# A new written-out order for a two-layer linear-attention kernel, with the first loads dealt anew to two queues

## The chip, the cores and the metric

The kernel runs on one core of one Trainium2 chip. The metric is device time in microseconds (us), the median over runs of the same program. Smaller is better.

## What is computed

Two layers, each an attention block A and a gated block B, on 2048 rows of 512 features in bfloat16. Both layers use the same weights. The attention has 32 heads of 16 features and no softmax over rows: a feature map of keys and queries (two softmaxes over 16 features) turns it into products.

```python
def A(x, wqkv, w_phi, wo):                       # H = 32 heads, Dh = 16
    q, k, v = split_heads(x @ wqkv)
    pq, pk = q @ w_phi, k @ w_phi                # per head, 16 x 16
    phi_q = concat(softmax(pq), softmax(-pq))
    phi_k = concat(softmax(pk), softmax(-pk))
    kv, z = phi_k.T @ v, phi_k.sum(rows)         # over all 2048 rows
    return merge_heads(phi_q @ kv / (phi_q @ z + 1e-6)) @ wo

def B(x, W_gate, W_up, W_down):                  # 512 -> 1376 -> 512
    return (relu(x @ W_gate) * (x @ W_up)) @ W_down

x = A_x
for layer in range(2):
    x = x + A(layernorm(x), A_wqkv, A_w_phi, A_wo)
    x = x + B(layernorm(x), B_W_gate, B_W_up, B_W_down)
```

## The kernel before

The 2048 rows are 16 tiles of 128 rows (t0 to t15), in four chunks of four tiles. X stays in SBUF for the whole run. `w_phi` is folded into the key and query weights once at the start: VectorE spreads it into block matrices `Wblk` by two products (L269), TensorE multiplies them with the transposed key weights `wkT` in four folds b0 to b3 of four matmuls each (L287), and the results are evacuated into `Wk2` by ScalarE (L249) or VectorE (L251). The same is done later for the query weights (`Wq2`), whose transposing load is L279.

A tile's way through the start of a layer: VectorE takes statistics (L311, aggregated in L313), GpSimd makes the scalars (L319, L321 the power -1/2, L368, L370), ScalarE (L382) or VectorE or GpSimd (both L394) normalises, and the normalised tile is transposed, either by TensorE (L403, with an evacuation; only for t0) or by a transposing DMA on SyncE's queue (L412 for one tile, L408 for two at once). Then TensorE makes keys (L575) and values (L516), ScalarE two exponentials of the keys (L580), VectorE sums them over the features (L546, or L552 and L556 for halves) and inverts the sums, VectorE and GpSimd scale (L595), and TensorE adds the tile to the running product of keys and values (L617). After the last tile's keys the queries (L659, L663, L674, L681, turned by L683) meet that product (L700); the quotient (L718, L720) is turned by DMA (L727, L733) or TensorE (L740), projected (L751) and added to X (L420, L424). The next normalisation leads into block B: gate and up matmuls (L466), their evacuation and product (L476, L479), down projection (L498).

Nothing is ordered by the compiler. Every step is an operation of a planner (`Plan.op`) with an engine, and `ORDER` is a written-out permutation of all 1867 operations; each engine, SyncE's DMA queue included, executes its operations in that order. `STEP` holds letters and digits per tile that say which engine does a step: `xn1` normalises in layer 0, `xm0` ("2": two tiles turned by one DMA, "1": each by its own), `ks` (how many of eight head groups GpSimd scales), `kr` and `qr` (how sums are made), `sA` and `sB` (for how many chunks ScalarE's square replaces VectorE's statistics), `ot` (which engine turns the quotient), `wake` (dummy matmuls on zeros at the start, L260). The first loads are not in the order; they are issued at the head of `setup`.

By the numbering of the operations, the queues begin like this before the change (K and V are a tile's keys and values):

- TensorE: 8 dummies, fold b0, 2 dummies, fold b1, dummy, fold b3, transposition of t0, dummy, fold b2, dummy, V t0, dummy, K t0, dummy, V t1, K t1, K t2
- ScalarE: evacuate b0, normalise t0, normalise t1, evacuate t0's transposition, evacuate b1 and b2, normalise t2, both exponentials of t0, normalise t3 and t4, one exponential of t1, V t0, the other of t1, one of t3, V t1
- VectorE: statistics of t0, both `Wblk` products, statistics of t1, t3, t2, evacuate b3, statistics of t5, t4, t6
- GpSimd, around tiles 6 and 7: (scalars of t8/t9 and t6/t7 mixed) power of t9, power of t7, normalise t7, last scalar of t6/t7
- SyncE: t1, t2, t3, the pair t4/t5, the query weights, the pair t6/t7

Of the kernel before, what the change touches and what calls it, by code (L numbers as in the profile page):

```python
# [9 lines left out]
D = 512  # L10
# [123 lines left out]
WF_IN, WK_IN, WV_IN, WQ_IN, LOADED = 3.6, 5.6, 8.25, 13.0, 13.0  # L134
X_IN = [3.25, 5.2] + [6.75] * 2 + [9.75] * 4 + [11.25] * 4 + [12.75] * 4
# [8 lines left out]
def setup(ctx, tc, A_x, A_wqkv, A_w_phi, A_wo, B_W_gate, B_W_up, B_W_down, out):  # L144
    nc = tc.nc
    st = KS()
# [11 lines left out]
    pl = st.pl = Plan()  # L158
# [3 lines left out]
    X = const.tile([P, T, D], BF16, name="X")  # L162
    xv = xf.rearrange("(t p) d -> p t d", p=P)
# [3 lines left out]
    wf = const.tile([P, NDB, DH], BF16, name="wf")  # L167
    nc.sync.dma_start_transpose(out=wkT[:], in_=A_wqkv[:, D:2 * D])
    nc.scalar.dma_start(out=X[:, 0:1, :], in_=xv[:, 0:1, :])
# [7 lines left out]
    wake = const.tile([P, 1], F32, name="wake")  # L177
# [86 lines left out]
def feature_weights(st):  # L264

    nc, pl = st.nc, st.pl
# [6 lines left out]
    for name, dst, off, at in (("Wk2", st.Wk2, D, WK_IN), ("Wq2", st.Wq2, 0, WQ_IN)):  # L273
        pl.rank("w" if off else "wq")
        if off:
            part, deps = (lambda m, b: st.wkT[:, b, m * P:(m + 1) * P]), []
        else:
            wqT = Buf("b4", [P, NDB, D], BF16)
            pl.op("SP", 2.0, lambda: nc.sync.dma_start_transpose(out=wqT[:], in_=st.wq_in),  # L279
                  reads=[("turns", 1)], writes=[(wqT, 0)], at=at, lat=3.0)  # L280
            part, deps = (lambda m, b: wqT[:, b, m * P:(m + 1) * P]), [(wqT, 0)]
# [406 lines left out]
def attention(st, c, pT, norm, L):  # L688
# [71 lines left out]
    "part0": "4111", "part1": "4111", "tB0": "A---", "tB1": "D-D-", "tA": "----", "wev": "AADDAAADADAAAAAA",  # L760
    "xn1": "AAAAADAPDAADAAAA", "turn": "A---", "wake": 19, "fuse0": "FFFA", "fuse1": "AFFF", "gate": 1, "sB0": 4,
# [6 lines left out]
}  # L768
ORDER = (
# [176 lines left out]
```

## Time and profile before

| | |
|---|---|
| Runs | 384.75 us median of 3 (384.26 to 385.19) |
| Profiled execution | 384.6 us, span 382.9 us |
| Busy TensorE, VectorE, ScalarE, GpSimd | 366.5, 274.9, 199.9, 136.6 us |
| Granted TensorE clock, mean of the span | 1.00 |
| Packets moved by DMA | 100065, 31.82 MB |

The profile is of one execution. Times in it are us from the start of the span. In a row of the timeline the first number is the start, the second the duration, then come engine, line, operation, what is written and read, and in brackets how long the engine had been idle and what ended the wait. ACTq and SPq are the DMA queues of ScalarE and SyncE. Rows that overlap on one engine are pipelined.

### The profile page before, as it was taken

The numbers are of one execution on the slowest core, as the hardware profiler recorded it, in microseconds if no ns is written. First come the engines' busy times: TensorE is split into PE (matmuls) and PEld (weight loads), VectorE is DVE, ScalarE is ACT, GpSimd is POOL, SyncE is SP. The second block draws the span as 40 slices with busy tenths as digits, with TensorE's granted clock in tenths as the row PEclk, the third lists the DMA queues.
The fourth block names the chain that finished last, engine by engine and source line by source line (L and its number), as shares of the span: only waits on it lengthen the run. The fifth ranks groups of instructions, "written<-read, shape, count | busy, mean of one in ns | idle before, by whom it ended". The sixth has DMA issues, their size and how long they took to land.

```text
span 382.9 us, 6693 instructions
## 1 busy us (share of the span) xinstructions
PE 366.5 (96%) x2384; PEld 190.5 (50%) x2417; DVE 274.9 (72%) x601; ACT 199.9 (52%) x428; POOL 136.6 (36%) x281
## 2 busy tenths in 40 slices
PE   7978988989989999999999989999999999999997
PEld 3334454756544544444454445576554544454443
DVE  6999999998875775556787878999974746333432
ACT  3799866924377621333777556995635432332100
POOL 4799775914343001133361344374531202000000
PEclk9999999999999999999999999999999999999999
DMA  8699647443872520017302122364784221310004
GB/s 243 162 146 267 148 110 140 90 86 68 161 123 44 98 41 3 0 28 119 74 2 42 27 44 43 62 119 87 143 146 96 57 41 15 69 41 2 0 5 134
DMA packets 100065, 31.82 MB, mean 83 GB/s; under 512 B 91488, under 2 KB 100032, under 8 KB 100032
## 3 DMA queue, kind: packets, MB, share of 16 engines
q1 hardware_dynamic: 96832, 28.75, 38.8%
q10 hardware_dynamic: 3200, 2.64, 2.3%
q8 instruction: 19, 0.31, 0.4%
q14 instruction: 14, 0.11, 0.1%
HBM read 7.39 MB, written 2.10 MB: 25 GB/s over the span
## 4 chain that ended last, share of the span: by engine, by line
PE 81%; DMA 9%; ACT 2%; DVE 2%; issue 2%; POOL 2%; SPq 0%; ACTq 0%; POOLq 0%; DVEq 0%
PE ps L466 36%; PE ps L498 16%; DMA b<-b 7%; PE ps L751 7%; PE ps L575 5%; PE ps L659 5%; PE ps L516 5%; PE ps L446 2%; PE q L700 2%; PE q L617 1%; DMA wf<-in_A_w_phi_dram 1%; ACT b L580 1%; DVE sk L556 1%; ACT b L382 1%; POOL b L595 0%
## 5 line engine op out<-in xcount | busy, mean ns | idle before, releaser
L476 ACT CAST b<-ps 128x512 bf16<-128x512 f32 (+2 forms) x100 | 47.7, 505 | 69.3 <-PE ps L466 69.1
L466 PE MATMUL ps<-b,wu 128*128 128x512 bf16 (+2 forms) x400 | 79.5, 336 | 0.5 <-DMA b<-b 0.5
L466 PE MATMUL ps<-b,wg 128*128 128x512 bf16 (+2 forms) x400 | 79.7, 336 | 0.0
L498 PE MATMUL ps<-wd,b 128*128 128x512 bf16 (+3 forms) x365 | 79.1, 366 | 0.5
L479 DVE SCALAR_TENSOR_TENSOR b<-ps,b 128x512 bf16<-128x512 f32 (+2 forms) x70 | 40.5, 605 | 36.5 <-PE ps L466 25.5
L595 POOL TENSOR_TENSOR b<-b,rk 128x1024 bf16<-128x1024 bf16 (+7 forms) x30 | 41.0, 1381 | 45.0 <-DVE rk L589 30.4
L498 PEld LDWEIGHTS <-b 128*128 128x128 bf16 (+1 forms) x374 | 35.4, 98 | 39.1 <-issue 0.2
L466 PEld LDWEIGHTS <-wu 128*128 128x128 bf16 x400 | 35.9, 98 | 32.5 <-DMA b<-b 0.8
L466 PEld LDWEIGHTS <-wg 128*128 128x128 bf16 x400 | 35.8, 98 | 31.5
L580 ACT ACTIVATE b<-ps 128x512 bf16<-128x512 f32 x64 | 35.9, 613 | 16.2 <-PE ps L575 15.8
L382 ACT ACTIVATE b<-X,ve,rstd 128x512 bf16<-128x512 bf16 x39 | 31.6, 823 | 16.4 <-POOL ve L370 16.4
L663 ACT ACTIVATE b<-ps 128x512 bf16<-128x512 f32 x64 | 34.9, 615 | 8.3 <-PE ps L659 7.2
L681 POOL TENSOR_TENSOR b<-b,rq 128x512 bf16<-128x512 bf16 x24 | 25.4, 1068 | 30.1 <-DVE rq L674 29.6
L575 PE MATMUL ps<-Wk,b 128*128 128x512 bf16 x125 | 31.8, 379 | 4.6 <-DMA b<-b 4.4
L420 DVE SCALAR_TENSOR_TENSOR X<-ps,X 128x512 bf16<-128x512 f32 x36 | 24.3, 681 | 16.0 <-PE ps L498 8.3
L424 DVE TENSOR_TENSOR X<-X,ps 128x512 bf16<-128x512 bf16 (+2 forms) x30 | 19.3, 648 | 21.7 <-PE ps L498 16.1
L334 ACT ACTIVATE sq<-X 128x512 bf16<-128x512 bf16 x36 | 22.9, 636 | 18.8 <-DVE X L420 18.5
L516 PE MATMUL ps<-wvt,b 128*128 128x512 bf16 x124 | 31.8, 379 | 0.9 <-DMA b<-b 0.6
L751 PE MATMUL ps<-wo,b 128*128 128x512 bf16 x117 | 31.1, 379 | 0.7
L659 PE MATMUL ps<-Wq,b 128*128 128x512 bf16 x122 | 30.2, 379 | 0.3
L546 DVE TENSOR_REDUCE sq<-b 128x64 f32<-128x1024 bf16 x19 | 22.5, 1199 | 0.0
L720 DVE TENSOR_TENSOR b<-q,dd 128x512 bf16<-128x512 f32 x32 | 21.8, 681 | 0.3
(86 smaller groups left out, 444.7 us busy)
## 6 DMA issues: line engine op xcount, KB each, us to landing
out_dram<-X SPq DMA_DIRECT2D x15, 128.0 KB, 1.8
X<-in_A_x_dram ACTq DMA_DIRECT2D x3, 512.0 KB, 7.1
b<-b SPq DMA_TRANSPOSE x92, 3.1
wu<-in_B_W_up_dram SPq DMA_DIRECT2D x8, 160.0 KB, 3.4
wg<-in_B_W_gate_dram SPq DMA_DIRECT2D x8, 160.0 KB, 3.6
wd<-in_B_W_down_dram SPq DMA_DIRECT2D x5, 256.0 KB, 3.9
wvt<-in_A_wqkv_dram ACTq DMA_DIRECT2D x1, 512.0 KB, 5.1
wo<-in_A_wo_dram SPq DMA_DIRECT2D x4, 128.0 KB, 3.2
```

What stands on the lines that cost most here:

```text
L382: pl.op("ACT", 0.72, lambda to=to, t=t, j=j: nc.scalar.activation(out=to(), in_=st.X[:, t, :], func=AF.Identity, scale=rstd[:, j:j + 1], b ...
L466: nc.tensor.matmul(ps[:], lhsT=wt[:, b, f * P:(f + 1) * P], rhs=xnT[:, lo:hi, b, :], start=(b == 0), stop=(b == NDB - 1))
L476: pl.op("ACT", 0.065 + 0.42 * share, lambda ups=ups, ru=ru: nc.scalar.copy(out=ru[:], in_=ups[:]), reads=[(ups, 0)], writes=[(ru, 0)])
L479: pl.op("DVE", 0.08 + 0.53 * share, lambda gps=gps, ru=ru, h=h, cs=cs: nc.vector.scalar_tensor_tensor(out=h[:, cs], in0=gps[:], scalar=0.0 ...
L498: nc.tensor.matmul(yps[:], lhsT=hs[f][:fsz, ti * P:(ti + 1) * P], rhs=st.wd[:fsz, f, cols], start=(f == 0), stop=(f == NFT - 1))
L516: nc.tensor.matmul(vp[:], lhsT=xnT[:, ti, kb, :], rhs=st.wvt[:, kb, :], start=(kb == 0), stop=(kb == NDB - 1))
L575: nc.tensor.matmul(ps[:], lhsT=xnT[:, ti, kb, :], rhs=w(kb), start=(kb == 0), stop=(kb == NDB - 1))
L580: pl.op("ACT", 0.49, lambda s=s, ek=ek, pk=pk: nc.scalar.activation(out=ek[:, :, s, :], in_=pk[:].rearrange("p (j x) -> p j x", j=8), func ...
L595: eng.tensor_tensor(out=phiK[:, lo:hi, :, :].rearrange("p j s (f h) -> p (j s) f h", h=4), in0=ek[:, lo:hi, :, :].rearrange("p j s (f h) - ...
L659: nc.tensor.matmul(pq[:], lhsT=xnT[:, ti, kb, :], rhs=st.Wq2[:, kb, :], start=(kb == 0), stop=(kb == NDB - 1))
L663: pl.op("ACT", 0.49, lambda s=s, eq=eq, pq=pq: nc.scalar.activation(out=eq[:, :, s, :], in_=pq[:].rearrange("p (j x) -> p j x", j=8), func ...
L751: nc.tensor.matmul(yps[:], lhsT=turned(b), rhs=st.wo[:, b, :], start=(b == 0), stop=(b == NDB - 1))
```

## The change

The loads at the head of `setup`, the planner's arrival times, the duration of one planned DMA, the letters of `STEP` and the whole of `ORDER` are new. `ORDER` has 1863 operations now.

```diff
-WF_IN, WK_IN, WV_IN, WQ_IN, LOADED = 3.6, 5.6, 8.25, 13.0, 13.0
-X_IN = [3.25, 5.2] + [6.75] * 2 + [9.75] * 4 + [11.25] * 4 + [12.75] * 4
+WF_IN, WK_IN, WV_IN, WQ_IN, LOADED = 3.35, 6.0, 8.3, 13.0, 13.0
+X_IN = [3.1, 4.7] + [6.8] * 2 + [9.8] * 4 + [11.3] * 4 + [12.8] * 4
...
+    nc.sync.dma_start(out=X[:, 0:1, :], in_=xv[:, 0:1, :])
     nc.sync.dma_start_transpose(out=wkT[:], in_=A_wqkv[:, D:2 * D])
-    nc.scalar.dma_start(out=X[:, 0:1, :], in_=xv[:, 0:1, :])
     nc.scalar.dma_start(out=wf[:], in_=A_w_phi.rearrange("(b j) d f -> (j d) b f", b=NDB, j=8))
     nc.scalar.dma_start(out=X[:, 1:2, :], in_=xv[:, 1:2, :])
...
-            pl.op("SP", 2.0, lambda: nc.sync.dma_start_transpose(out=wqT[:], in_=st.wq_in),
-                  reads=[("turns", 1)], writes=[(wqT, 0)], at=at, lat=3.0)
+            pl.op("SP", 2.3, lambda: nc.sync.dma_start_transpose(out=wqT[:], in_=st.wq_in),
+                  reads=[("turns", 1)], writes=[(wqT, 0)], at=at, lat=2.9)
...
-    "part0": "4111", "part1": "4111", "tB0": "A---", "tB1": "D-D-", "tA": "----", "wev": "AADDAAADADAAAAAA",
-    "xn1": "AAAAADAPDAADAAAA", "turn": "A---", "wake": 19, "fuse0": "FFFA", "fuse1": "AFFF", "gate": 1, "sB0": 4,
-    "sB1": 3, "sA": 2, "xB0": "ADADDAADDADADDDD", "xB1": "DADAAADDAAAAADAA", "xA": "AADDDDDAAADAAAAA",
-    "xm0": "11222211", "xmB0": "12222112", "xmB1": "22222221", "xm1": "12221212", "om0": "11112222",
-    "om1": "11222222", "ev0": "AAAAAAAAAAAAAAAA", "ev1": "AAADDAADAAAAAAAA", "ks0": "7888076880873788",
-    "ks1": "4321818154616442", "kr0": "H112121121122222", "kr1": "P111121112122212", "qm0": "DPDDDDDDDDPDDDPD",
-    "qm1": "DDDDPPDDDDPDDPDD", "qr0": "2111H1122121P1PP", "qr1": "111P112122111112", "qs0": "PPPPPPPPDDDPDPPD",
-    "qs1": "DDPDPPPPPPPPPPPP", "ot0": "DDDD------DDAA--", "ot1": "--A-DDAD---DD--A",
+    "part0": "4111", "part1": "4111", "tB0": "A---", "tB1": "D-D-", "tA": "----", "wev": "ADDDAAADADAAAAAA",
+    "xn1": "AAAAADAPDAADAAAA", "turn": "A---", "wake": 18, "fuse0": "FFFA", "fuse1": "AFFF", "gate": 1, "sB0": 2,
+    "sB1": 3, "sA": 3, "xB0": "ADADDADDDADADDAD", "xB1": "DADAAADDDAAAADAA", "xA": "AADDDDDAAAAAAAAA",
+    "xm0": "21122111", "xmB0": "12222112", "xmB1": "22222221", "xm1": "11222212", "om0": "11112222",
+    "om1": "11222222", "ev0": "AAAAAAAAAAAAAAAA", "ev1": "AAADDADDAAAAAAAA", "ks0": "6888076880873788",
+    "ks1": "4322018154616442", "kr0": "H112121121122222", "kr1": "P111121112222212", "qm0": "DPDDDPDDDDPDDDPP",
+    "qm1": "DDDDPPDDDDPDDPDD", "qr0": "1111H1122121P1PP", "qr1": "1112112122111112", "qs0": "PPPPPPPPDDDPDPPP",
+    "qs1": "DDPDPPPDPDPPPPPP", "ot0": "DDDD------DDADAA", "ot1": "----DDAD---DA--A",
...
-    131, 144, 139, 143, 145, 129, 135, 130, 0, 1, 148, 149, 2, 3, 9, 4, 5, 150, 138, 10, 147, 152, 11, 13, 134, 12,
+    136, 140, 133, 145, 147, 131, 0, 138, 148, 1, 149, 146, 141, 137, 2, 132, 4, 3, 9, 10, 150, 5, 157, 153, 13,
...
```

By the numbering, the queues begin like this after it:

- TensorE: 12 dummies, folds b3, b1, b0, b2, transposition of t0, K t0, 3 dummies, V t0, K t1, V t1, K t2, V t2, K t3, dummy, K t4
- ScalarE: normalise t0, evacuate b0, b1, b2, normalise t1, evacuate t0's transposition, normalise t2 and t3, both exponentials of t0, normalise t4, V t0, one exponential of t1, V t1, normalise t6, the other of t1, one of t2, both of t3
- VectorE: statistics of t0, one `Wblk` product, statistics of t1, the other product, statistics of t2, t3, evacuate b3, statistics of t4, t5, t6
- GpSimd, around tiles 6 and 7: power of t7, last scalar of t6/t7, normalise t7, power of t9
- SyncE: t1, t2, t3, t5, t4, the query weights, the pair t6/t7

Counted over the whole run, TensorE loses one dummy and one transposition of a tile's quotient (`ot1`, t2), VectorE gains 9 operations (four more statistics with their aggregates among them), ScalarE loses 6, GpSimd 8, and SyncE gains 3 transposing DMAs.

184 rows, old and new, of the table ORDER are left out of this document.

## The prediction

> **What bounds the kernel now.** I read the page first, then the busy time of each engine in stretches of 10 us, then the timelines of the first 40 us engine by engine, and last the groups of instructions by line. From the page:
>
> ```profile
> span 382.9 us, 6693 instructions
> ...
> PE 366.5 (96%) x2384; PEld 190.5 (50%) x2417; DVE 274.9 (72%) x601; ACT 199.9 (52%) x428; POOL 136.6 (36%) x281
> ```
>
> TensorE is busy for 366.5 of 382.9 us, so all that any order can win from idle TensorE is 16.4 us. The stretches say where they lie (columns: us, then busy us of PE, PEld, DVE, ACT, POOL, with counts):
>
> ```profile
> 10.00:20.00 10.00, 9.07 (x40) 3.60 (x41) 9.28 (x25) 7.33 (x15) 7.18 (x18) 1.00 0.67 156
> ...
> 20.00:30.00 10.00, 8.27 (x54) 4.19 (x54) 9.39 (x19) 9.68 (x20) 9.35 (x17) 1.00 1.03 153
> ...
> 30.00:40.00 10.00, 8.89 (x67) 4.27 (x67) 9.89 (x15) 10.00 (x20) 9.90 (x6) 1.00 1.05 245
> ...
> 50.00:60.00 10.00, 8.73 (x99) 5.20 (x100) 10.00 (x16) 6.62 (x14) 7.65 (x8) 1.00 0.32 67
> ...
> 220.00:230.00 10.00, 8.88 (x71) 4.47 (x70) 7.64 (x15) 5.07 (x8) 4.90 (x16) 1.00 0.24 42
> ```
>
> In the stretches from 10 to 60 us TensorE is idle for 0.93, 1.73, 1.11 and 1.27 us, while VectorE is busy for 9.28 to 10.00 of each 10 us and ScalarE for up to 10.00. That is the key and query phase of layer 0: the vector engines set its pace, and TensorE waits for them. Between 220 and 230 us 1.12 us are lost, the most of any stretch after 110 us. So the change can win something in the first third, little after that, and it can lose anywhere.
>
> **The start: three loads and what hangs on them.** Timeline of the first 14 us (start, duration, engine, line):
>
> ```profile
> 0.78 0.39 ACTq L169 DMA_DIRECT2D X<-in_A_x_dram  x1
> ...
> 0.79 1.42 SPq L168 DMA_TRANSPOSE wkT<-in_A_wqkv_dram  x1
> ...
> 1.20 0.45 ACTq L170 DMA_DIRECT2D wf<-in_A_w_phi_dram  x1
> ...
> 1.24 3.60 PE L260 MATMUL ps<-zero 128*128 128x512 bf16 x8 [1.24 <-DVE zero L176]
> ...
> 5.32 0.19 POOL L370 TENSOR_TENSOR ve<-u,rstd 128x1 f32<-128x1 f32 x1
> ...
> 5.52 0.76 DVE L269 TENSOR_TENSOR Wblk<-M,wf 128x256 bf16<-128x256 bf16 x2 [1.16 <-DMA wf<-in_A_w_phi_dram]
> ...
> 6.20 0.69 DVE L311 BATCH_NORM_STATS2 bnst<-X 128x6 f32<-128x512 bf16 x1
> ...
> 7.02 0.66 DVE L311 BATCH_NORM_STATS2 bnst<-X 128x6 f32<-128x512 bf16 x1
> ...
> 6.43 0.59 PE L287 MATMUL ps<-Wblk,wkT 128*128 128x128 bf16 x4 [1.60 <-DVE Wblk L269]
> ...
> 7.54 0.81 ACT L382 ACTIVATE b<-X,ve,rstd 128x512 bf16<-128x512 bf16 x1
> ...
> 8.55 0.81 ACT L382 ACTIVATE b<-X,ve,rstd 128x512 bf16<-128x512 bf16 x1 [0.20 <-POOL ve L370]
> ...
> 9.39 5.94 SPq L412 DMA_TRANSPOSE b<-b  x3
> ...
> 9.56 0.39 PE L287 MATMUL ps<-Wblk,wkT 128*128 128x128 bf16 x4
> ...
> 10.02 1.08 ACT L249 CAST Wk<-ps 128x512 bf16<-128x512 f32 x2
> ...
> 11.27 1.03 PE L575 MATMUL ps<-Wk,b 128*128 128x512 bf16 x4
> ...
> 13.14 1.04 PE L516 MATMUL ps<-wvt,b 128*128 128x512 bf16 x4 [0.62 <-DMA b<-b]
> ```
>
> ```profile
> wkT<-in_A_wqkv_dram SPq DMA_TRANSPOSE x1, 4.8
> ...
> wf<-in_A_w_phi_dram ACTq DMA_DIRECT2D x1, 16.0 KB, 4.2
> ```
>
> w_phi (`wf`) is issued second on ScalarE's queue at 1.20 and needs 4.2 us to land. The two VectorE products that spread it (L269) start at 5.52 and the next statistics follow at 6.20, so one product occupies 0.34 us. The first fold of the key weights (L287) waits for the second product and starts at 6.43.
>
> After the change w_phi is issued first, at about 0.78 instead of 1.20: it lands 0.42 us earlier, and the first product starts at about 5.1. X's first tile goes first on SyncE's queue at about 0.79, as early as before, and its statistics stay where they are. The key weights' transposing load stands behind it: one issue of 0.39 us (the row at 0.78) later, so it lands near 0.79 + 0.39 + 4.8 = 6.0. That costs nothing, because the second product below is later still; without that cover it would cost 0.4 us.
>
> But the new order puts tile 1's statistics between the two products. Statistics with their aggregate take 0.82 us (from 6.20 to the next at 7.02). So the second product ends at 5.1 + 0.34 + 0.82 + 0.42 = 6.7 (0.42 is the rest of the pair's 0.76), and the first fold starts near 6.75: 0.3 us later than before. Tile 1's statistics are 0.7 us earlier for the same reason.
>
> TensorE's dummies: twelve instead of eight stand ahead of the folds. Eight took 3.60 us, 0.45 each, so twelve end by 1.24 + 12 x 0.45 = 6.6: they fit before the fold is ready and cost nothing, and they close the hole from 4.84 to 6.43. If w_phi landed earlier than I think they would cost up to the 0.2 us by which they pass 6.43.
>
> The sixteen fold matmuls now run in one piece. A dummy has 512 columns and takes 0.45 us, a fold has 128 and should take a quarter, 0.11. Four took 0.59 us at 6.43 but 0.39 at 9.56, and four matmuls of 512 columns took 1.03 at 11.27, so 0.26 each with their latency: TensorE was about half as fast at first as later. So sixteen folds take 1.8 us at the slow pace and 0.9 at the fast one, and end at 8.5 or 7.7. The trace of before cannot show which it will be. The Trainium skill, "TensorE: Matmul & The Clock Gate", Part 1, says that full speed comes after one whole free-running window of about 3.4 us of steady matmuls, and that twelve gapless dummies would fill such a window: by that rule the folds run at the fast pace, and the rival of a slow start below loses most of its chance. The forecast's own sum would be the same by both, since its start term is zero.
>
> ScalarE's order: tile 0's normalisation now comes ahead of the weight evacuations. Its scalars were ready at 5.32 + 0.19 = 5.51, but it ran at 7.54 behind the evacuation: 2.0 us are won for that one operation. Then come three evacuations of 0.54 us each (1.08 for two), the first of them for the third fold, so from about 7.5 at the fast pace or 8.3 at the slow one, and only then tile 1's normalisation: at about 9.1 or 9.9, against 8.55 before. Its transposing DMA on SyncE's queue follows, at 9.39 before, and the tile was used at 13.14, so 3.75 us later: 13.7 to 14.5 after. Tile 0's keys come one normalisation (0.81) and one evacuation (0.54) after that point, at 10.4 to 11.2 against 11.27, because the new order has keys ahead of values. So tile 0's keys are 0.1 to 0.9 us earlier, tile 1 is 0.5 to 1.3 us later. What waits for tile 1's keys is their sum on VectorE:
>
> ```profile
> 16.83 0.61 ACT L580 ACTIVATE b<-ps 128x512 bf16<-128x512 f32 x1
> ...
> 19.60 1.18 DVE L546 TENSOR_REDUCE sk<-b 128x64 f32<-128x1024 bf16 x1
> ```
>
> Before, the second exponential of tile 1 ended at 17.44 and VectorE came to the sum at 19.60: 2.2 us of room, filled with statistics of later tiles. That room hides 1.3 us. I take the start as 0, with ends of -0.9 (tile 0's keys) and +1.3 (tile 1's delay in full).
>
> **Tiles 6 and 7.** These rows are POOL's, ScalarE's, SyncE's and TensorE's:
>
> ```profile
> 17.52 0.71 POOL L321 TENSOR_TENSOR rstd<-ve,mhalf 128x2 f32<-128x2 f32 x1
> ...
> 18.35 2.09 POOL L394 TENSOR_SCALAR b<-X,mv,rstd 128x512 bf16<-128x512 bf16 x1
> ...
> 20.41 0.19 POOL L370 TENSOR_TENSOR ve<-u,rstd 128x2 f32<-128x2 f32 x1
> ...
> 20.93 1.56 ACT L382 ACTIVATE b<-X,ve,rstd 128x512 bf16<-128x512 bf16 x2
> ...
> 21.81 3.96 SPq L408 DMA_TRANSPOSE b<-b  x2
> ...
> 26.53 1.90 PE L575 MATMUL ps<-Wk,b 128*128 128x512 bf16 x7 [1.19 <-DMA b<-b]
> ...
> 36.68 1.04 PE L575 MATMUL ps<-Wk,b 128*128 128x512 bf16 x4 [0.99 <-DMA b<-b]
> ```
>
> Here the old order has a knot. POOL normalises tile 7 (18.35, 2.09 us) before it makes tile 6's last scalar (20.41); ScalarE normalises tile 6 only at 20.93; the pair's transposing DMA leaves at 21.81, and TensorE waits 1.19 us for it at 26.53. The new order makes that scalar ahead of the long POOL operation, drops tile 9's power (0.71 us) behind tile 7's, and moves tile 6 up on ScalarE ahead of tile 2's and 3's exponentials. Tile 7 then starts on POOL near 17.5 and the pair is ready near 19.6, 2 us earlier. SyncE is free then, if the query weights' load keeps its place: tiles 4 and 5 are turned by two DMAs instead of one, which adds one issue of about 1.2 us ahead of it. So the wait of 1.19 us goes. What is late next are the vector engines, full from 20 to 40 us: VectorE idles 0.61 + 0.11 us there. I take -0.4, between 0 and -1.19. The wait of 0.99 us at 36.68 is for a later tile, with four DMAs for tiles 10 to 15 unchanged and two for 10 and 11 in place of one; I leave it, with 0 to -0.99 for the range.
>
> **The phase up to the first gate and up matmuls.** I counted each engine's instructions ahead of the first one in both orders. ScalarE has 102 in both, POOL 72 in both, VectorE 131 before and 128 after. The difference by kind:
>
> ```profile
> L546 DVE TENSOR_REDUCE sk<-b 128x64 f32<-128x1024 bf16 x16 | 19.1, 1204 | 3.7 <-ACT b L580 3.7
> ...
> L556 DVE TENSOR_REDUCE sk<-b 128x32 f32<-128x512 bf16 x29 | 18.5, 661 | 2.8 <-ACT b L580 2.7
> ...
> L674 DVE TENSOR_TENSOR rq<-sq 128x32 bf16<-128x32 f32 x25 | 5.9, 239 | 0.0
> ...
> L718 DVE RECIPROCAL dd<-q 128x32 f32<-128x32 f32 x32 | 11.1, 347 | 3.7 <-PE q L700 3.5
> ```
>
> Two sums of L556 and one of L546 change places (-2 x 0.66 + 1.20), one product L674 moves to POOL (-0.24), and one reciprocal L718 comes later (-0.35): -0.7 us on the engine that sets the pace. Some of it falls in its idle time. I take -0.3.
>
> **TensorE's own work.** One transposition of four 128-column matmuls in layer 1 becomes a DMA (`ot1`, tile 2): at the fast pace's half of 0.11 that is -4 x 0.055 = -0.22 us, in the full part of the span. One dummy fewer would be as much again, but it stood where TensorE waited anyway, so 0.
>
> **Statistics moved between engines.** `sB0` 4 to 2 and `sA` 2 to 3 turn four net tiles from ScalarE's square to VectorE's statistics:
>
> ```profile
> L311 DVE BATCH_NORM_STATS2 bnst<-X 128x6 f32<-128x512 bf16 x28 | 18.5, 677 | 0.4 <-DMA X<-in_A_x_dram 0.3
> ```
>
> VectorE gets 4 x 0.68 = 2.7 us more, ScalarE loses as many squares. This lies between 110 and 230 us, where VectorE's stretch of 220 to 230 us is 7.64 busy, so 2 us in 10 are free. I cost it at 0. If that cover is gone, it shows as a wait like the one at the layer boundary, where tile 12's chain ends in a DMA:
>
> ```profile
> 225.91 1.04 PE L575 MATMUL ps<-Wk,b 128*128 128x512 bf16 x4 [1.01 <-DMA b<-b]
> ```
>
> 1.01 us is the price of one such wait. This one stays: in both orders three whole down projections stand between tile 12's own and its keys. I keep 0 to +1.0 for one new wait after 110 us.
>
> **Sum.** 0 (start) - 0.4 (tiles 6, 7) - 0.3 (VectorE) - 0.22 (transposition) = -0.9 us. The profiled execution took 384.6 us (span 382.9 and 1.7 around it), so 383.7 us; the median of the runs is 384.75, 0.15 above the profiled one, and I don't correct for that. Against the median that is -0.27%. About 0.2% (0.77 us) is what a measurement of this kernel can tell from no change.
>
> **Rivals.** *The gain is swallowed:* the search used its own list of durations and arrivals (w_phi at 3.35 us, where the trace has it after 5.4), so its order is no better than the old one on the chip, and the knot's 1.19 us is given back a few microseconds later to VectorE and ScalarE, which are full. Only the transposition is left: 384.6 - 0.22 = 384.4. For it speaks the VectorE stretch of 50 to 60 us, 10.00 busy; against it, that VectorE itself has less to do.
>
> *Tile 1 is late and stays late:* the folds run at half speed, tile 1's normalisation sits behind three evacuations, and the 1.3 us are not hidden, because VectorE runs out of statistics before tile 1's exponentials arrive. From then on every vector step up to the first gate matmul is 1.3 us late, and the knot's gain is lost in it: 384.6 + 1.3 - 0.22 = 385.7, and 386.7 with one new wait of 1.0 after 110 us. It decides when the second exponential of tile 1 ends more than 2.2 us later than 17.44. Against it speaks that room; for it, that ScalarE must now also evacuate tile 1's values and normalise tile 6 ahead of that exponential. Tile 6's last scalar comes near 17.4, so the exponential ends near 17.4 + 0.81 + 0.61 = 18.8, which uses 1.4 of the 2.2 us even when tile 1 is on time.
>
> **Chances.** Forecast 0.45, swallowed 0.2, late tile 0.35. The forecast's own range is 381.3 (all of -0.9 at the start and -1.19 and -0.99 at the two waits, with -0.22) to 384.0. The whole range is 381.3 to 387.0: the upper end is the late tile with one new wait and a little of a second. Faster 0.45, same 0.2, slower 0.35 follow directly.
>
> **What would show it.** Right: w_phi's product at about 5.1, folds in one piece from 6.7, tile 0's normalisation at 5.5, tile 6 and 7's pair leaving SyncE before 20.5, no wait of TensorE of 1 us near 26, first gate or up matmul about 0.7 us earlier, and TensorE's idle time after 110 us unchanged. Wrong: VectorE idle for more than 1 us between 10 and 20 us, tile 1's keys after 14.5, or new DMA waits of TensorE of about 1 us after 110 us.

## The result, and the profile after

The changed kernel takes 388.17 us (median of six runs, 387.78 to 388.8) against 384.37 us for the kernel before, a ratio of 1.0097 with an interval of 1.0082 to 1.0112. It is slower by 3.8 us, beyond the forecast of 383.7 us and beyond the range. The profiled execution took 387.8 us; its page:

```profile
span 386.1 us, 6719 instructions
...
PE 369.1 (96%) x2412; PEld 191.1 (49%) x2412; DVE 277.5 (72%) x606; ACT 195.5 (51%) x418; POOL 133.7 (35%) x273
```

The span is 3.2 us longer. Timeline of its start:

```profile
0.79 0.48 ACTq L170 DMA_DIRECT2D wf<-in_A_w_phi_dram  x1
...
1.24 3.00 SPq L169 DMA_TRANSPOSE wkT<-in_A_wqkv_dram  x1
1.24 4.73 PE L260 MATMUL ps<-zero 128*128 128x512 bf16 x12 [1.24 <-DVE zero L176]
...
4.15 0.41 DVE L269 TENSOR_TENSOR Wblk<-M,wf 128x256 bf16<-128x256 bf16 x1
...
5.30 0.39 DVE L269 TENSOR_TENSOR Wblk<-M,wf 128x256 bf16<-128x256 bf16 x1
...
5.78 0.81 ACT L382 ACTIVATE b<-X,ve,rstd 128x512 bf16<-128x512 bf16 x1 [1.94 <-POOL ve L370]
...
10.48 1.89 PE L287 MATMUL ps<-Wblk,wkT 128*128 128x128 bf16 x16 [4.51 <-DMA wkT<-in_A_wqkv_dram]
...
11.98 1.56 ACT L249 CAST Wk<-ps 128x512 bf16<-128x512 f32 x3 [5.39 <-PE ps L287]
...
14.27 5.84 SPq L412 DMA_TRANSPOSE b<-b  x4
...
14.78 1.89 PE L575 MATMUL ps<-Wk,b 128*128 128x512 bf16 x4 [1.99 <-ACT b L249]
```

The steps at the head came near the forecast: w_phi's first product at 4.15 (forecast 5.1), tile 0's normalisation (L382) at 5.78 (5.5), the dummies done before 6 (6.6). Then TensorE stands still for 4.51 us, until 10.48, and the row says for what: the key weights. VectorE's second product, the cover that was to hide them, had begun at 5.30. ScalarE's first evacuation waits 5.39 us behind the folds, tile 0's keys come at 14.78 instead of 11.27, and the normalised tiles leave on SyncE's queue from 14.27 on instead of 9.39. The list of waits has it in one line (us in total, times, longest):

```profile
PE ps L287 <- DMA wkT<-in_A_wqkv_dram: 4.5, 1, 4.5
```

The loads, with us from issue to landing, of the changed kernel and then of the kernel before:

```profile
X<-in_A_x_dram ACTq DMA_DIRECT2D x3, 512.0 KB, 9.5
...
wf<-in_A_w_phi_dram ACTq DMA_DIRECT2D x1, 16.0 KB, 2.3
wkT<-in_A_wqkv_dram SPq DMA_TRANSPOSE x1, 9.2
```

```profile
X<-in_A_x_dram ACTq DMA_DIRECT2D x3, 512.0 KB, 7.1
```

The same 512 KB of key weights need 9.2 us, not 4.8, and X's large loads 9.5, not 7.1; w_phi gained (2.3 for 4.2), and so did X's tile 1 (3.1 for 4.2). Busy time by stretch, for the row of 10 to 20 us shown of before:

```profile
10.00:20.00 10.00, 7.53 (x35) 3.86 (x36) 6.05 (x15) 6.64 (x11) 4.93 (x14) 0.55 0.62 170
```

VectorE falls from 9.28 to 6.05 us and the granted clock from 1.00 to 0.55. The first gate or up matmul comes 1.9 us later; these two rows are of before and of after:

```profile
72.62 0.83 PE L466 MATMUL ps<-b,wu 128*128 128x128 bf16 x12
```

```profile
74.48 0.61 PE L466 MATMUL ps<-b,wu 128*128 128x128 bf16 x8
```

### The profile page after: what moved, and what is told of

Read it like the earlier page. It is cut to its first block, busy times and chain, and to the rows that moved or that the text cites. A ratio compares the mean times of both kernels' runs of the same rounds, so it can differ in the third digit from the quotient of the medians.

```text
span 386.1 us, 6719 instructions
## 1 busy us (share of the span) xinstructions
PE 369.1 (96%) x2412; PEld 191.1 (49%) x2412; DVE 277.5 (72%) x606; ACT 195.5 (51%) x418; POOL 133.7 (35%) x273
## 4 chain that ended last, share of the span: by engine, by line
PE 75%; DVE 13%; DMA 6%; ACT 2%; issue 2%; POOL 1%; SPq 0%; POOLq 0%
PE ps L466 34%; PE ps L498 17%; PE ps L751 6%; PE ps L659 4%; PE ps L575 4%; DMA b<-b 4%; PE ps L516 3%; PE ps L446 2%; DMA wkT<-in_A_wqkv_dram 2%; DVE sk L556 2%; DVE rk L589 2%; DVE sk L546 2%; DVE sq L546 2%; PE q L700 2%; DVE b L595 1%
## 5 line engine op out<-in xcount | busy, mean ns | idle before, releaser
L498 PE MATMUL ps<-wd,b 128*128 128x512 bf16 (+4 forms) x374 | 79.6, 366 | 0.0
L595 POOL TENSOR_TENSOR b<-b,rk 128x1024 bf16<-128x1024 bf16 (+7 forms) x29 | 40.1, 1396 | 43.1 <-ACT b L476 13.1
L424 DVE TENSOR_TENSOR X<-X,ps 128x512 bf16<-128x512 bf16 (+2 forms) x34 | 22.1, 653 | 33.4 <-PE ps L498 23.4
L382 ACT ACTIVATE b<-X,ve,rstd 128x512 bf16<-128x512 bf16 x39 | 32.1, 834 | 15.8 <-POOL ve L370 14.4
L663 ACT ACTIVATE b<-ps 128x512 bf16<-128x512 f32 x64 | 34.2, 615 | 10.7 <-PE ps L659 10.5
L575 PE MATMUL ps<-Wk,b 128*128 128x512 bf16 x128 | 32.9, 387 | 4.4 <-DMA b<-b 2.4
L681 POOL TENSOR_TENSOR b<-b,rq 128x512 bf16<-128x512 bf16 x23 | 24.6, 1070 | 19.1 <-DVE rq L674 15.6
L334 ACT ACTIVATE sq<-X 128x512 bf16<-128x512 bf16 x32 | 20.3, 635 | 18.6 <-DVE X L420 18.4
L420 DVE SCALAR_TENSOR_TENSOR X<-ps,X 128x512 bf16<-128x512 f32 x32 | 21.6, 678 | 5.9 <-PE ps L498 5.1
L341 POOL TENSOR_SCALAR u<-mv 128x2 f32<-128x2 f32 (+1 forms) x20 | 4.6, 234 | 55.8 <-DVE X L420 55.4
L546 DVE TENSOR_REDUCE sq<-b 128x64 f32<-128x1024 bf16 x20 | 23.7, 1201 | 0.0
```

The source lines that it names most:

```text
L498: nc.tensor.matmul(yps[:], lhsT=hs[f][:fsz, ti * P:(ti + 1) * P], rhs=st.wd[:fsz, f, cols], start=(f == 0), stop=(f == NFT - 1))
L546: pl.op("DVE", 1.13, lambda: nc.vector.tensor_reduce(out=sums[:].rearrange("p j s h -> p (j s) h"), in_=e[:].rearrange("p j s (f h) -> p ( ...
L575: nc.tensor.matmul(ps[:], lhsT=xnT[:, ti, kb, :], rhs=w(kb), start=(kb == 0), stop=(kb == NDB - 1))
L595: eng.tensor_tensor(out=phiK[:, lo:hi, :, :].rearrange("p j s (f h) -> p (j s) f h", h=4), in0=ek[:, lo:hi, :, :].rearrange("p j s (f h) - ...
L663: pl.op("ACT", 0.49, lambda s=s, eq=eq, pq=pq: nc.scalar.activation(out=eq[:, :, s, :], in_=pq[:].rearrange("p (j x) -> p j x", j=8), func ...
```

## Experiments

The first theory, *loads*: the new dealing of the loads makes the key weights late, and that is the whole loss. Its rival, *order*: the new order is the worse one on the chip. A diff below is against the changed kernel unless it says otherwise. `wk`, `x0`, `x1`, `x23`, `wf` stand for the loads of key weights, X's tile 0, tile 1, tiles 2 and 3, and w_phi; SP and ACT for the queues.

**e1_old_loads: new order, old loads**

```diff
-SP: x0, wk     ACT: wf, x1, x23, ...
+SP: wk         ACT: x0, wf, x1, x23, ...
```

> The changed kernel with the three first loads dealt as before the change (SyncE's queue: the key weights alone; ScalarE's: X's first tile, then w_phi); order and letters stay new. Theory 'loads' (the key weights' load, which landed 9.2 us after its issue instead of 4.8, is the whole loss): it lands near 5.6 again, the first fold starts at 6.4 to 6.8, and the time is 383.6 to 385.0 us. Theory 'order' (the new order is itself slower, the late load only moves where it shows): 386.5 us or more.

382.96 us against 384.72, ratio 0.9969 (0.9953 to 0.9984): faster than before, and below what either theory gave, although the folds began at 7.32, later than *loads* had it. Rows of its timeline (TensorE and SyncE):

```profile
7.32 1.05 PE L287 MATMUL ps<-Wblk,wkT 128*128 128x128 bf16 x16 [1.35 <-DVE Wblk L269]
...
19.17 5.07 SPq L408 DMA_TRANSPOSE b<-b  x2
...
70.10 0.61 PE L466 MATMUL ps<-b,wu 128*128 128x128 bf16 x8
```

The key weights landed 4.7 us after issue. The folds run in one piece at the fast pace, 1.05 us for sixteen; pair 6/7 leaves SyncE at 19.17 instead of 21.81; the first gate matmul comes 2.5 us ahead of before.

**e2_new_loads: old order, new loads** (diff against before: e1's in reverse)

> The kernel before with the three first loads dealt as after the change; order and letters stay old. Theory 'loads': the first fold starts near 10.5 us instead of 6.4, and the time is 387.5 to 388.5 us. Theory 'order': the old order has w_phi's product and the fold early and other work to fill with, so 384.4 to 385.5 us.

388.31 us, ratio 1.0107 (1.0085 to 1.0128), key weights 9.8 us to landing. With e1 this settles loads against order: the loads cost about 1.1% under the old order and 1.3% under the new one (1.0097 against 0.9969), and the order is worth about 0.3%.

Next: why is the load late? *Place*: it stands behind x0 on its queue. *Competition*: loads of ScalarE's queue are in flight beside it. Nine runs moved the loads about.

**e3_keys_first**

```diff
-SP: x0, wk
+SP: wk, x0
```

> The changed kernel with the two loads on SyncE's queue exchanged: key weights first, X's first tile behind; w_phi still first on ScalarE's queue. Within theory 'loads': if the place behind X's first tile makes the key weights late, they land at 5.6 to 6.2 us and the time is 384.5 to 385.5 us. If it is the X loads, which now reach the DMA engines at 2.5 us instead of 4.5 because w_phi no longer holds ScalarE's queue, they land at 7.5 to 9 us and the time is 386 to 387.5 us.

388.05 us, ratio 1.0095 (1.0073 to 1.0117): even longer than *competition* gave, but for another reason. The key weights landed after 5.3 us, as *place* had it, or a little earlier; but now x0 needed 6.5, its statistics held VectorE's products back, and the folds waited for these:

```profile
11.78 1.87 PE L287 MATMUL ps<-Wblk,wkT 128*128 128x128 bf16 x16 [5.54 <-DVE Wblk L269]
```

**e4_shield**

```diff
-ACT: wf, x1, ...
+ACT: x1, wf, ...
```

> The changed kernel with X's second tile ahead of w_phi on ScalarE's queue, so that w_phi's 512 small packets hold up the later X loads again; SyncE's queue as changed (X's first tile, then key weights). If competition with the X loads makes the key weights late, they now land at 6.5 to 7.5 us, and the time is 385 to 386 us. If their place behind X's first tile does it, they land near 10 us as after the change, and the time stays at 387.5 to 388.5 us.

387.87 us, scattered (385.57 to 389.39), ratio 1.0079 (1.005 to 1.0108); key weights 10.9 us. Both are what *place* gave; w_phi is no shield behind x1.

**e6_keys_alone**

```diff
-SP: x0, wk     ACT: wf, x1, ...
+SP: wk         ACT: wf, x0, x1, ...
```

> The changed kernel with the key weights alone on SyncE's queue and on ScalarE's w_phi first, X's first tile second: w_phi no longer holds up the X loads, but nothing stands ahead of the key weights. Theory 'place' (a transposing load behind another load on its queue is slow): they land 5.3 to 6.0 us after the start and the time is 382.5 to 384 us. Theory 'competition' (X loads that start before the key weights are done slow them): they land at 7.5 us or later and the time is 386 us or more.

384.98 us, ratio 1.0014 (0.9996 to 1.0032); key weights 5.9 us, the landing of *place*, in a time above its 382.5 to 384. The folds begin at 8.58, waiting for a product, since x0 is late behind w_phi.

**e7_hold_x and e9_hold_all** put a one-column copy on ScalarE that reads the key weights, so that the loads behind it wait for them: in e7 behind x1, in e9 behind w_phi.

> The changed kernel, its queues as changed (X's first tile, then key weights on SyncE's), but with all loads after X's second tile issued by ScalarE only once the key weights have landed (one copy of a column of them stands ahead). Theory 'place': the key weights still land 9 us or more after their issue, and the time is 388 us or more. Theory 'competition': they land 4.7 to 5.3 us after their issue, near 6.2 us; the later X tiles come 1 to 2 us late, and the time is 383.5 to 385.5 us.

> X's first tile ahead of the key weights on SyncE's queue as in the changed kernel, but every load of ScalarE's queue behind w_phi is held until the key weights have landed, so that nothing of X but its first tile can be in flight beside them. If a place behind another load on its own queue is what makes the transposing load late (place), it still lands 9 to 11 us after its issue. If it is late because packets of X were in flight when its own began and shared the engines (competition), it lands 4.7 to 5.7 us after its issue, with 256-byte packets near 18 ns. The kernel's time is no measure here: X comes some 3 to 8 us later, 388 to 394 us.

Neither is the test that was meant. In both traces only X's three 512-KB loads left after the copy; x1, x23 and the 512 KB of value weights went out at 1.27 to 2.39 us all the same. The key weights took 10.3 and 10.5 us (388.22 us, ratio 1.0111 with 1.0084 to 1.0138; and 388.47 in one run). What they show: the three large X loads are not needed for the loss.

**e10_late_alone** is e6 with a small memset of VectorE into `wkT` ahead of its load, which then starts at 1.48.

> The key weights alone on SyncE's queue, but begun about 1 us later than before (behind a small memset of VectorE), and ScalarE's queue with w_phi, X's first tile and all of X's other loads. If place behind another load is the cause, it lands 4.7 to 5.7 us after its own issue, as in the run with the keys alone. If the cause is that loads of X are in flight when its packets begin, it lands 8 to 10 us after its issue, and its 256-byte packets take 24 ns or more on average; time 386 to 389 us.

Key weights 6.5 us, between the two forecasts (385.25 us, one run). A late start alone does not make the 9 to 11 us.

**e12_only_x0** makes the hold real: GpSimd writes a column into each place of X's tiles 1 to 15 and of the value weights, reading the key weights.

```diff
 SP: x0, wk     ACT: wf
+nc.gpsimd.tensor_copy(out=X[:, 1:16, 0:1], in_=wkT[:, 0, 0:15].unsqueeze(2))
+nc.gpsimd.tensor_copy(out=wvt[:, :, 0:1], in_=wkT[:, 0, 0:4].unsqueeze(2))
 ACT: x1, x23, ...
```

> The changed kernel, but all of ScalarE's loads behind w_phi (X from tile 1 on, and the value weights) wait until the key weights have landed, here by small writes of GpSimd into their places that read the key weights first; only X's first tile, ahead on SyncE's queue, and w_phi are in flight beside them. The earlier two runs with a hold kept back only X's three 512-KB loads, and 128 + 256 + 512 KB were still in flight. Place (a load ahead of it on its own queue is enough): the key weights land 9 to 11 us after issue, SyncE's issue takes 2.7 to 3.2 us. Competition (loads of the other queue in flight): they land 5 to 6 us after issue, 256-byte packets near 18 ns, issue near 1.4 us. The time is no measure (X comes late): 388 to 396 us.

Behind x0, with w_phi and nothing else beside it, the load takes 5.0 us. So place alone does not make it late. (Its one run took 385.6 us, less than expected and less than the changed kernel, although X's loads left only from 6.59 us on.)

Where the time goes can be read from the packets (q1 is SyncE's queue, q10 ScalarE's; packets, MB, and the time that they took as a share of all 16 engines). The key weights are 2048 packets of data, and 32 that carry next to nothing come last. First the changed kernel from 3.1 to 7.84 us, in which all the data falls:

```profile
q1 hardware_dynamic: 2048, 0.52, 78.5%
q10 hardware_dynamic: 388, 0.37, 35.5%
```

Then e12 from 2.75 to 5.85 us, data and last packets with hardly anything beside them, and the changed kernel from 9 to 12 us, nearly X alone:

```profile
q1 hardware_dynamic: 2080, 0.52, 93.7%
```

```profile
q10 hardware_dynamic: 1002, 0.99, 109.6%
```

At these paces the key weights take 3.1 us and X's 0.37 MB would take another 1.1; one after the other that is an estimate of 4.2 us. Side by side they took 4.7. The Trainium skill, "DMA: Bandwidth & Descriptors", section "Issuing engines are not separate DMA queues", says that transfers of all queues run on the same 16 DMA engines and interleave. The trace agrees that both go on at once (2048 and 388 packets here), and sharing at the paces above gives all but 0.5 us.

But the data was complete at 7.84, and the load landed only at 10.44. In between, the changed kernel from 7.84 to 9.4 and from 9.4 to 9.8 us, and for comparison the kernel before from 2.2 to 5 us:

```profile
q10 hardware_dynamic: 574, 0.57, 110.1%
```

```profile
q1 hardware_dynamic: 32, 0.00, 5.3%
```

```profile
q1 hardware_dynamic: 2080, 0.52, 85.1%
```

For 1.6 us nothing ran on SyncE's queue while X's loads filled the engines; then came the last 32 packets, which in the kernel before come together with the last of the data. So the landing at 10.44 instead of 5.59 is made up of data that begins 0.8 us later (3.10 instead of 2.27), takes 2.2 us longer (4.74 instead of 2.55), and of last packets that are done 1.9 us after it.

**e13_wf_ahead and e14_no_spacer** start from e11 below, with its quick old loads.

```diff
 # e13                              # e14
-SP: wk      ACT: x0, wf, x1, ...   ACT: x0, wf, x1, x23, ...
+SP: wf, wk  ACT: x0, x1, ...       ACT: x0, x1, x23, wf, ...
```

> The run with the second product ahead of tile 1's statistics, but w_phi first on SyncE's queue with the key weights behind it, and X's first tile first on ScalarE's. Place: the key weights land 9 to 11 us after issue although the load ahead of them is only 16 KB, the folds begin near 11 us, time 387 to 389 us. If instead X's loads overtaking is decided by which packets begin first, X's first three loads now begin ahead of the key weights too and nothing is told apart by the landing, but SyncE's issue near 1.4 us would speak against place. If neither holds (w_phi is too small to matter, and X's loads matter little): landing 5.5 to 6.5 us, folds near 7 us, time 382 to 384 us.

> The fastest version so far (new order, second product first, key weights alone and first on SyncE's queue at 0.79 us), but w_phi behind X's tiles 0 to 3 on ScalarE's queue instead of behind tile 0, so that 512 KB of X follow each other without w_phi's 512 small packets between them. If the key weights came quickly there because w_phi kept the rest of X back (spacer), they now land 6.5 to 10 us after their issue, w_phi late too, and the folds begin after 8 us: 385 to 389 us. If being first and alone on its queue at 0.79 us is enough (first wins), they land at 4.7 to 5.5 us as before, w_phi lands near 6 to 7 us, and the folds begin near 8 us because of the products: 383 to 385.5 us.

e13: 389.68 us, ratio 1.0149 (1.013 to 1.0169), key weights 11.3 us, the latest of all, behind a load of 16 KB; *place* gave 9 to 11. e14: 385.09 us, ratio 1.0011 (0.9994 to 1.0028), key weights 6.0 us, w_phi late, folds at 9.02: neither forecast, but between them. All landings together (us from issue to landing, one profiled execution each):

| Key weights on SyncE's queue | X beyond tile 0 in flight | us |
|---|---|---|
| first | held back by w_phi's packets (before, e1, e11, e8, e15) | 4.8, 4.7, 4.8, 4.9, 4.9 |
| first | yes (e3, e6, e14, e10) | 5.3, 5.9, 6.0, 6.5 |
| behind another load | no (e12) | 5.0 |
| behind another load | yes (after, e2, e5, e7, e16, e9, e4, e13; e5 and e16 are below) | 9.2, 9.8, 9.8, 10.3, 10.3, 10.5, 10.9, 11.3 |

Either condition alone costs up to 1.7 us; both together cost 4.4 to 6.5. That is shown. In the packets the last line differs from the others in one more point: in all eight of its loads the last packets are done 0.8 to 1.9 us after the data, in the other rows together with it. Why the two conditions do this together is not shown: SyncE's issue, too, takes 2.5 to 3.25 us whenever a load is ahead of it and 1.42 when it is first, in e12 also (2.50), where the landing is quick.

The remaining question was how much of the loss is the late start, and how much the half clock that follows.

**e5_keep_warm** puts eleven more dummies behind the twelve.

> The changed kernel with eleven more dummy matmuls behind the twelfth, so that TensorE does not stand idle while it waits for the key weights. If the half speed after that wait is a part of the loss, the sixteen folds take 0.9 to 1.1 us instead of 1.89, tile 0's keys 1.03 instead of 1.89, and the time falls by 1 to 1.7 us, to 386.5 to 387.2 us. If the late load alone sets the pace (the vector engines catch up), the time stays at 387.7 to 388.5 us.

388.39 us, ratio 1.0117 (1.0096 to 1.0138). No answer: the key weights were later still (9.8 us), a hole of 3.28 us stayed, and the clock fell in it. Stretches of 8 to 11 and 11 to 14 us:

```profile
8.00:11.00 3.00, 0.00 (x0) 0.00 (x0) 1.50 (x4) 0.00 (x0) 1.04 (x4) 0.98 1.11 309
11.00:14.00 3.00, 2.31 (x20) 2.05 (x20) 2.31 (x4) 1.46 (x4) 1.04 (x4) 0.50 1.11 349
```

**e16_keys_late_warm**: twenty more there, and ten in the next hole, ahead of tile 0's keys.

> The changed kernel with its late key weights, but twenty more dummies at the end of the first twelve, to last until about 10.3 us, and ten more between tile 0's transposition and its keys, so that TensorE's clock stays at 1.00 while the key weights are as late as before. If the loss is the late start alone (late only), 387.5 to 388.5 us. If the clock of 0.50 from 11 to 17 us is a good part of it (clock), folds take 1.05 instead of 1.89 us, tile 0's keys 1.03 instead of 1.89, and the time falls by 1 to 2 us, to 386 to 387 us.

The trace has no stretch of half clock; folds 1.07 us, keys 1.04:

```profile
11.63 1.07 PE L291 MATMUL ps<-Wblk,wkT 128*128 128x128 bf16 x16 [1.75 <-DMA wkT<-in_A_wqkv_dram]
...
15.32 1.04 PE L579 MATMUL ps<-Wk,b 128*128 128x512 bf16 x4 [0.23 <-ACT b L249]
```

387.21 us, scattered (383.78 to 389.38), ratio 1.007 (1.0039 to 1.0101). Most of the loss is still there, with the key weights at 10.3 us and the folds from 11.63 on instead of 10.48. So the larger part is lateness; the clock may be the other 0.3%, but this interval and the changed kernel's overlap. The mean granted clock of each run says a little more: in e16 the six runs at 0.999 or 1.00 have a median of 386.8 us, and the three at 0.995 to 0.996 took 387.9 to 389.4. In e1 the one run at 1.00 took 382.0 us, six at 0.995 to 0.996 have a median of 382.8, and five at 0.991 one of 383.9.

**e11_product_first**: e1, and VectorE's second product ahead of tile 1's statistics (operation 150 ahead of 9).

> The new order with the old loads, and on VectorE the second product with w_phi ahead of tile 1's statistics, which wait for X until 5.96 us in the run of the new order with the old loads. The second product then ends near 5.9 instead of 7.2 us and the sixteen folds begin near 6.1 instead of 7.32 us. If the start of the folds still sets the end, the time falls by up to 1.2 us, to 381.8 to 382.8 us, ratio 0.993 to 0.996. If the arrival of X's later tiles and VectorE's work set the end by then (VectorE is busy all of 20 to 70 us), nothing measurable is left of it: 382.7 to 383.5 us, ratio 0.9965 +- 0.0015.

382.56 us, ratio 0.9937 (0.9912 to 0.9962). Folds from 6.42. Against e1 the gain is not certain, since the intervals overlap.

**e15_filled_hole**: e11, with ten dummies ahead of tile 0's keys, where TensorE waits 2.39 us and the clock falls.

> The fastest version so far (new order, old loads, second product first), with ten dummies between the transposition of tile 0 and tile 0's keys, where TensorE waits 2.39 us for the evacuation and the granted clock falls to 0.50 between 11 and 13 us. If the slow clock sets the pace there (clock), the clock stays at 1.00 from 10 to 20 us, tile 0's keys take 1.03 instead of 1.87 us, and the end comes 0.5 to 1.5 us earlier: 381.0 to 382.0 us. If VectorE (busy 9.72 of the 10 us there) sets the pace (late only), the clock stays at 1.00 and the time does not change: 382.2 to 383.0 us.

381.59 us, ratio 0.9922 (0.9894 to 0.9949): the fastest version, 0.8% below the kernel before. Stretch of 10 to 20 us, of e11 and then e15:

```profile
10.00:20.00 10.00, 9.65 (x37) 3.90 (x38) 9.72 (x25) 7.70 (x14) 8.26 (x20) 0.83 0.70 160
```

```profile
10.00:20.00 10.00, 9.49 (x43) 4.01 (x45) 9.86 (x26) 8.13 (x15) 8.61 (x20) 1.00 0.77 164
```

The clock is held and the median falls by 1.0 us, as *clock* expected; the intervals overlap here too. That the clock is the reason is not shown: in e11 itself the three runs at 0.999 or 1.00 took 382.6 to 383.2 us, no less than the five at 0.996 (381.8 to 382.6).

**e8_knot**: the kernel before with only six moves in its order, those around tiles 6 and 7 (operations 48 to 51 and 53 ahead of 61, 52 ahead of 191).

> The kernel before, loads and letters old, with six operations of its order moved: tile 6's last scalar and tile 7's normalisation on GpSimd ahead of the scalars of tiles 8 and 9, and tile 6's normalisation on ScalarE ahead of tile 2's and 3's exponentials. The prediction's reading: the pair of tiles 6 and 7 leaves SyncE at 19.5 to 20.5 us instead of 21.8, TensorE's wait of 1.2 us at 26.5 goes, and the time falls by 0.4 us (0 to 1.2). Rival 'swallowed': the wait goes, but the first gate or up matmul stays at 72.6 us, and the time at 384.4 to 384.8 us.

384.15 us, ratio 1.0002 (0.9986 to 1.0019). The pair leaves SyncE at 20.46 instead of 21.81, TensorE's waits at 26.53 and 36.68 are gone and the first gate matmul is 0.9 us earlier in the profile, but nothing measurable is left in the time.

## Why the prediction was wrong

The step that failed is one sentence of the start: the key weights' load "lands near 0.79 + 0.39 + 4.8 = 6.0. That costs nothing, because the second product below is later still". It landed at 1.24 + 9.2 = 10.4. The working carried over a duration, 4.8 us, that held for a load first on its queue while w_phi's packets kept X back behind tile 0. The change removed both conditions at once: x0 went ahead of the key weights, and w_phi, now first, let X's loads run beside them. The price given for a lost cover, 0.4 us, was that of one issue alone.

The other steps, one by one:

- *w_phi and the products.* Forecast 5.1 for the first; it began at 4.15, because w_phi's own load shortened to 2.3 us. The error had the same root, a duration taken as fixed, and cost nothing.
- *Dummies and folds.* Twelve fit, as forecast (1.24 to 5.97). That folds in one piece would then run fast was right where they came in time: 1.05 us in e1, the fast pace's 0.9 within 0.15. The trace of e1 agrees with the rule of the Trainium skill, "TensorE: Matmul & The Clock Gate", Part 1, cited there. In e11 the folds begin at 6.42, the clock is full only from 7.00 on, and they take 1.31 us. With the key weights late the same folds took 1.89 us.
- *Tiles 6 and 7.* The pair left at 23.76 in the changed kernel, not at 19.6; with the old loads it left at 19.17 and the wait of 1.19 us at 26.53 was gone. The mechanism was right and hung on the start. Alone (e8) it is worth less than can be measured, which is the time of the rival *swallowed*, though in e8's profile the gain was still there at the first gate matmul.
- *The order as a whole.* Forecast -0.9 us. With the old loads it gave -2.0 us in the profiled execution, and the ratio of 0.9969 is about -1.2 us: right in sign, and somewhat too small. The terms for VectorE and for the dropped transposition were not tested one by one.
- *After 110 us.* One new wait was kept at 0 to +1.0. The time came, between 270 and 290 us, and with the old loads too, but as two waits: 0.69 us for a product of VectorE (L720) and 0.41 us for a turned quotient's DMA. These rows of before, after and e1 give it: TensorE idle 0.11, 1.10 and 1.16 us of 20.

```profile
270.00:290.00 20.00, 19.89 (x142) 11.10 (x141) 16.08 (x41) 9.12 (x22) 6.32 (x11) 1.00 0.82 149
```

```profile
270.00:290.00 20.00, 18.90 (x133) 10.11 (x132) 16.10 (x40) 8.33 (x19) 8.63 (x16) 1.00 0.88 145
```

```profile
270.00:290.00 20.00, 18.84 (x134) 10.06 (x133) 15.30 (x43) 6.35 (x16) 3.92 (x8) 1.00 0.72 119
```

- *Tile 1 late and stays late* forecast 385.7 from half-speed folds and a long queue of evacuations. Its condition was met: tile 1's second exponential began at 22.75 instead of 16.83, 5.9 us later (1.7 in e1, with the old loads). The slow folds were there, but as a consequence; it was the folds themselves that came late, and every tile with them, so this rival did not name the cause either.

Of the 3.2 us in the span, 1.86 are there at the first gate matmul (74.48 against 72.62), and the waits of TensorE that the traces list behind it sum to 2.8 us before and 3.8 after, 1.0 more. The last 0.3 us I have not traced. That only 1.9 us of a start delayed by 3.5 to 4 us reach the gate matmuls is the order's own gain and no idle time that swallows the rest: in e1, with the same order, tile 0's keys come 3.8 us earlier (10.99) and the first gate matmul 4.4 us earlier (70.10), and the order alone puts that matmul 2.5 us ahead of before.

## What to carry to other kernels

A load's time from a trace belongs to its place: before moving it, write down what is ahead of it on its queue and what else is in flight while it runs, and reprice it if the move changes either. A small load with many small packets can be the thing that keeps large loads off an urgent one, so moving it first may cost more than its own earlier landing brings. Test the loads and the order of a change apart: here one lost 1.3% and hid a gain of 0.3%.

## What was not expected of the hardware

The transposing load was late in full only where it stood behind another load on its queue and plain loads were in flight, and then a good part of the delay came after its data: 32 last packets that waited 1.6 us in the changed kernel while X's loads filled the engines.

The clock fell after rather short holes. In e11 TensorE idled 2.39 us ahead of tile 0's keys, which then took 1.87 us for four matmuls instead of 1.03; in e6 a hole of 2.58 us was followed by folds of 1.75 us; but in e14 the folds behind a hole of 2.47 us still took 1.05:

```profile
8.58 1.75 PE L287 MATMUL ps<-Wblk,wkT 128*128 128x128 bf16 x16 [2.58 <-DVE Wblk L269]
```

```profile
9.02 1.05 PE L287 MATMUL ps<-Wblk,wkT 128*128 128x128 bf16 x16 [2.47 <-DVE Wblk L269]
```

What decides is where the hole lies. In every trace that records a change, the granted clock changes only at the ends of stretches of 3.41 us that follow one another without a gap (in the changed kernel it is full from 5.26 to 8.67, one stretch, and half from there to 18.91, three). Three such stretches of e1 (behind the stretch stand its length and TensorE's busy time; the granted clock is the third number from the end), and then one each of e14 and e11:

```profile
5.25:8.67 3.42, 1.99 (x24) 1.23 (x21) 2.96 (x9) 1.29 (x2) 1.56 (x5) 1.00 1.10 348
8.67:12.08 3.41, 1.09 (x5) 0.51 (x6) 2.95 (x7) 3.41 (x7) 2.54 (x10) 1.00 1.10 344
12.08:15.49 3.41, 3.41 (x10) 1.01 (x9) 2.96 (x9) 2.64 (x5) 2.88 (x7) 0.50 0.53 109
```

```profile
6.65:10.06 3.41, 1.04 (x19) 1.07 (x20) 1.92 (x5) 0.99 (x2) 0.22 (x1) 1.00 1.13 323
```

```profile
7.00:10.41 3.41, 1.02 (x18) 0.85 (x16) 2.65 (x7) 2.86 (x6) 2.77 (x11) 1.00 1.10 350
```

Over all stretches of these seventeen traces the full clock fell after each one in which TensorE was busy for 1.42 us or less, and after none with 1.75 us or more. The fall comes at the end of the stretch: in e11 0.06 us after the hole, so that the keys were slow; in e1 the same hole of 2.39 us ended 1.09 us before it, and the keys still took 1.04 us; in e14 the folds were just done. Where the stretches lie differs from trace to trace (one ends at 8.67 in e1, at 7.00 in e11), so whether the work right behind a hole of this length is slow is chance.

The Trainium skill, "TensorE: Matmul & The Clock Gate", Part 1, has the clock fall after one idle window of about 3.4 us. The length agrees (3.41 us). That the stretch has to be idle does not: e11's held 1.02 us of matmuls and the clock fell at its end. In this kernel a hole of 2.4 us was enough.
